# The opening of an attention-and-experts kernel: k's first load in halves on SyncE, the table load ahead of the gate weights, the gate matrix behind the first PV

## The chip, the cores and the metric

The kernel runs on one core of a Trainium2 chip. The metric is the device time of one execution in microseconds (us); a measurement gives the median of several runs. The engines are called PE (TensorE), DVE (VectorE), ACT (ScalarE), POOL (GpSimd) and SP (SyncE, which here only issues DMA).

## The reference

Two stages follow each other. The first is grouped-query attention: 8 batches, 16 query heads, 4 key/value heads, 384 positions, head size 64. The second sends each of the 3072 tokens to one of 16 experts, chosen in two steps (a group of four, then an expert in it).

```python
k = np.repeat(k, group, axis=1); v = np.repeat(v, group, axis=1)
scores = scale * np.matmul(q, k.transpose(0, 1, 3, 2))
attn = np.exp(scores - np.max(scores, axis=-1, keepdims=True))
attn = attn / (np.sum(attn, axis=-1, keepdims=True) + 1e-09)
x = np.matmul(attn, v)          # to (3072 tokens, 1024)
...
g_logits = x @ w_group; g_idx = argmax(g_logits)       # 4 groups
e_logits = xg @ w_expert[g]; e_idx = argmax(e_logits)  # 4 experts of the group
h = np.maximum(x[mask] @ w1[g, e], 0.0)
out[tokens] = (g_w * e_w)[:, None] * (h @ w2[g, e])
```

## The kernel before, in words

The order of the instructions on every engine is written out by hand (`manual_schedule`), and every engine takes its own in that order.

**Attention.** A batch is worked in 24 units: 4 key/value heads ("groups") of 6 key chunks of 64 positions. For unit u, `score(u)` makes eight PE rows of scores (L310) into one of two "s" buffers of PSUM, and ACT writes their exponential as tile `e` (L316). `pv(u)` multiplies `e` with v (L329) and accumulates over the six units of a group in one "o" buffer of PSUM. `run` goes over the units: `score(u + 2)`, `pv(u)`, `tail(u)`, and then what a table of inserts says for this u. `tail` adds pairs of `e` on POOL (L336), has DVE reduce four sums of a group (L343) and evacuates the group's result. Sums over keys are then collected (`collect`, L405), multiplied out on PE (`sums`, L415), inverted (L419), spread (L426) and applied (L435).

**PSUM.** There are two "o" buffers. `ps_tile("o")` takes them in turn; `ps_tile("x")` takes the one that the current group's PV does not use. The first `pv` of a group takes the next buffer in turn, and so waits until whoever holds it has been read out: at the first PV of the second group (u = 6) this is the reader of the last "x" tile before it, which is `gate_matrix_b`'s `wgd` cast on DVE (L239).

**The opening.** Batch 0 can't wait for a DMA transpose, so its q and k are loaded as they are, cast to bf16, transposed on PE against an identity and evacuated (`first_k`, L254; `first_q`, L262; evacuation L245 on ACT or L247 on DVE). SP issues k's first half of the heads (L157), then v (L150), then k's other half of the heads (L173). ACT issues q's first two heads one after the other (L159), then the gate weights of the group and of the experts (L161, L162), and then takes its first exponential on a one-column tile, which brings its table load ahead of the work (L164). POOL issues the other heads of q (L170). While PE waits for data it runs matmuls on ones (`fill`, L273).

**The gate.** `gate_matrix_a` transposes the gate weights on PE (L225) and has DVE copy them to `wg` (L227) and add pairs to `wgs` (L231). `gate_matrix_b` multiplies `wgs` with a folded identity (L236) and has DVE cast the result to `wgd` (L239). Both serve the gate and a guess, from the mean of v, at which expert's weights will be wanted first (`first_guess`, `first_pick` at units 13 and 15: a chain of small DVE operations, L540 to L586, among them L580, which marks the expert). POOL then reads the guess and fetches these weights (`first_fetch`, L560).

After that come, batch by batch, the expert's two matrix products (L622, L633) with the next batch's attention between them.

Of the kernel before, what the change touches and what calls it, by code (L numbers as in the profile page):

```python
# [9 lines left out]
F32 = mybir.dt.float32  # L10
# [4 lines left out]
ACT = mybir.ActivationFunctionType  # L15
# [3 lines left out]
def kernel(  # L19
# [11 lines left out]
    nc = tc.nc  # L31
    P = 128
    B, Hq, S, D = q.shape
# [3 lines left out]
    G, Eg = moe_w1.shape[0], moe_w1.shape[1]  # L37
    F = moe_w1.shape[3]
    NE = G * Eg
    KQ = DM // P  # L40
    KG = KQ // Hkv
# [4 lines left out]
    NC = S // H2  # L46
# [14 lines left out]
    gpool = ctx.enter_context(tc.tile_pool(name="gate", bufs=1))  # L61
# [7 lines left out]
    def ps_tile(which, shape=None, dtype=F32):  # L69
        if which == "x":  # L70
            which = f"o{1 - turn['o']}"
        else:
            turn[which] = 1 - turn[which]
            which += str(turn[which])
        return psum.tile(shape or [P, 2, 512], dtype, name="ps_" + which)
# [3 lines left out]
    NK = Hkv // 2 * NC  # L79
    k16, qraw, vraw, qT, kT = {}, {}, {}, {}, {}  # L80

    def rows(x):
        return x.rearrange("h (p c) d -> (h p) (c d)", c=NC).rearrange("(a p) n -> p a n", p=P)
# [26 lines left out]
    def new_qT(b):  # L110
        qT[b] = xpool.tile([P, KQ * SC, P], BF16, name="qT")

    def new_kT(b):
        kT[b] = xpool.tile([P, NK, P], BF16, name="kT")
# [26 lines left out]
    q0f = stage[:, :4 * NQ].bitcast(F32).rearrange("p (a n) -> p a n", n=NQ)  # L141
    k0f = stage[:, 4 * NQ:8 * NQ].bitcast(F32).rearrange("p (a n) -> p a n", n=NQ)
# [5 lines left out]
    def load_v0(g0, g1):  # L148
        for r in range(2):
            nc.sync.dma_start(out=vraw[0][r * H2:(r + 1) * H2, g0:g1],  # L150
                              in_=v[0, g0:g1].rearrange("h (p c) d -> p h (c d)", c=NC))

    onesb = cpool.tile([P, 4 * P], BF16)
    ones1 = cpool.tile([P, P], BF16)
    nc.vector.memset(ones1, 1.0)
    nc.vector.memset(onesb, 1.0)
    nc.sync.dma_start(out=k0f[:, 0], in_=rows(k[0])[:, 0])  # L157
    for m in range(KG):
        nc.scalar.dma_start(out=q0f[:, m], in_=rows(q[0])[:, m])  # L159
    load_v0(0, 1)  # L160
    nc.scalar.dma_start(out=wraw[:KQ], in_=moe_w_group.rearrange("(a p) g -> a (p g)", p=P))  # L161
    nc.scalar.dma_start(out=wraw[KQ:], in_=moe_w_expert.rearrange("g (a p) e -> (g a) (p e)", p=P))  # L162
    early = gpool.tile([P, 1], F32, name="early")
    nc.scalar.activation(early, onesb[:, :1], ACT.Exp)  # L164
    id128f = cpool.tile([P, P], F32)
    make_identity(nc, id128f)
    id128b = cpool.tile([P, P], BF16)
# [1 line left out]
    for g in range(1, Hkv):  # L169
        nc.gpsimd.dma_start(out=qraw[0][:, KG * g:KG * (g + 1)],  # L170
                            in_=rows(q[0])[:, KG * g:KG * (g + 1)])
# [44 lines left out]
    def index_constants():  # L216
        nc.vector.tensor_copy(out=eidx, in_=eidx_i)
        nc.vector.tensor_scalar(eback, eidx, -1.0, float(NE - 1), op0=ALU.mult, op1=ALU.add)
        nc.vector.tensor_copy(out=pidx, in_=pback_i)

    def gate_matrix_a():
        pe = ps_tile("o")[:, 0, :Eg * 5 * KQ].rearrange("p (e n) -> p e n", e=Eg)
        wv = wraw.rearrange("a (p e) -> a e p", e=Eg)
        for e in range(Eg):
            nc.tensor.transpose(out=pe[:, e], in_=wv[:, e, :],  # L225
                                identity=id128f[:5 * KQ, :5 * KQ])
        nc.vector.tensor_copy(  # L227
            out=wg[:, :, :NW].rearrange("p k (a e) -> p e a k", e=Eg),
            in_=pe.rearrange("p e (a k) -> p e a k", k=KQ))
        pk = pe.rearrange("p e (a g t) -> p t g a e", a=5, t=KG)[:, 0]  # L230
        nc.vector.tensor_add(out=wgs.rearrange("p g (a e) -> p g a e", e=Eg), in0=pk,  # L231
                             in1=wg[:, 1::2, :NW].rearrange("p g (a e) -> p g a e", e=Eg))
# [10 lines left out]
    def evac(eng, out_, in_):  # L243
        if eng is nc.scalar:
            eng.copy(out=out_, in_=in_)  # L245
        else:
            eng.tensor_copy(out=out_, in_=in_)  # L247

    def first_k(gp, which, eng):
        lo = gp * NC  # L250
        pt = ps_tile(which, [P, 16, P], BF16)
        for i in range(NC):
            for s in range(2):
                nc.tensor.transpose(out=pt[s * D:(s + 1) * D, i, :], in_=k16[0][:, lo + i],  # L254
                                    identity=id128b)
        evac(eng, kT[0][:, lo:lo + NC, :], pt[:, :NC, :])

    def first_q(i0, n, which, eng):
        pt = ps_tile(which, [P, 16, P], BF16)
        for i in range(n):  # L260
            a, c = (i0 + i) // SC, (i0 + i) % SC
            nc.tensor.transpose(out=pt[:, i, :], in_=qraw[0][:, a, c * P:(c + 1) * P],  # L262
                                identity=id128b)
        evac(eng, qT[0][:, i0:i0 + n, :], pt[:, :n, :])

    def first_scores():
        new_kT(0)
        new_qT(0)
        warm = ps_tile("o")

        def fill(n):
            for i in range(n):
                nc.tensor.matmul(out=warm[:, i % 2, :], lhsT=onesb[:, :P], rhs=onesb, start=True,  # L273
                                 stop=True)

        for i in range(4):
            nc.tensor.matmul(out=warm[:, i % 2, :P], lhsT=ones1, rhs=ones1, start=True, stop=True)
        fill(6)
        nc.vector.tensor_copy(out=k16[0][:, :NC].rearrange("p c d -> p (c d)"), in_=k0f[:, 0])
        nc.scalar.copy(out=qraw[0][:, 0], in_=q0f[:, 0])  # L280
        nc.vector.tensor_copy(out=qraw[0][:, 1], in_=q0f[:, 1])
        first_k(0, "s", nc.scalar)
        first_q(0, SC, "s", nc.vector)
        first_q(SC, SC, "o", nc.vector)
        fill(2)

    def cast_k():
        nc.gpsimd.tensor_copy(out=k16[0][:, NC:NK].rearrange("p c d -> p (c d)"), in_=k0f[:, 1])
# [378 lines left out]
    def do(f, *a):  # L667
        return lambda: f(*a)

    gate_constants()
    first_scores()
    index_constants()
    at = {0: Attn(0), 1: Attn(1)}
    at[0].start()
    gate_matrix_a()
    state, weights = {}, {}

    new_qT(1)  # L680
# [45 lines left out]
    def second_scale():  # L726
        scale_x(0, 2, spread(0, 2), nc.gpsimd)

    GB = KG * SC
    a = at[0]  # L730
    a.run(0, NU, {
        1: [do(first_q, GB, GB, "x", nc.vector)],
        3: [cast_k],
        4: [gate_matrix_b, do(sum_v, 0, nc.gpsimd)],
        6: [do(collect, 0, 0, 1)],
        7: [do(first_q, 2 * GB, 2 * GB, "x", nc.vector)],
        8: [do(first_k, 1, "x", nc.vector)],
        10: [do(sums, 0, 0, 1, "x"), do(normalise, 0, 0)],
        13: [first_guess],
        14: [do(cast, 0, 0)],  # L740
# [20 lines left out]
    pt = ps_tile("x")  # L761
# [125 lines left out]
    for c in range(SC):  # L887
# [5 lines left out]
        for i, (n0, n1) in enumerate(parts):  # L893
# [8 lines left out]
            for j, (ps, x) in enumerate(halves(c)):  # L902
                eng = nc.scalar if j and i % 2 == 0 else nc.sync
# [5 lines left out]
    with tc.For_i(0, n_left, 1):  # L909
# [27 lines left out]
        x = xb[B]  # L937
        w1, w2 = fetch1(er), fetch2(er)
        m = gpool.tile([P, B, SC, NE], F32, name="pm")
# [51 lines left out]
```

The softmax here doesn't subtract the row's maximum and nothing guards it: scores larger than these inputs give would overflow.

## Time and profile before

| what | value |
|---|---|
| time, median of 3 runs | 366.86 us (366.44 to 367.07) |
| span of the profiled execution | 366.1 us |
| PE busy | 354.2 us (97%) |
| DVE, ACT, POOL busy | 275.7, 230.2, 160.5 us |
| first scores on PE (L310) | from 6.73 us |
| gate weights' transposes (L225) | 7.26 to 7.93 us |
| wgd cast (L239) | 13.28 to 13.69 us |
| k's second load: issue, and POOL's cast of it (L288) | 4.90 us, 14.35 us |

The page gives, for one execution, how long each engine was busy, and a chain of waits: followed back from the last instruction, at each step to what released it. An engine that is busy nearly all the time sets the end where it leads the chain; a wait of another engine costs only where the chain goes through it. Times in views are counted from the start of the span. A line such as L310 is the line of the kernel before.

### The profile page before, as it was taken

Reading aid. Unit: us, or ns where it says so; the run is one execution under the profiler, and the core shown is the slowest. Engines: PE = TensorE matmul, PEld = TensorE weight load, DVE = VectorE, ACT = ScalarE, POOL = GpSimd, SP = SyncE. Lnnn points to the kernel's source line nnn. Section 1 sums busy time; section 2 is a strip of 40 time slices with the busy share of each in tenths; the row PEclk is TensorE's granted clock in tenths of the full one; section 3 lists DMA queues with packets and bytes.
Section 4 is the critical chain, followed back from the end, with each engine's and each line's share of the span. In section 5 each row is a group of like instructions: output and inputs, shape, how many; then the busy total and the mean of one; then the engine's idle time right before and its main releaser. Section 6 shows DMA issues by size and latency. Waiting matters only on the chain.

```text
span 366.1 us, 9424 instructions
## 1 busy us (share of the span) xinstructions
PE 354.2 (97%) x3907; PEld 183.2 (50%) x3907; DVE 275.7 (75%) x506; ACT 230.2 (63%) x300; POOL 160.5 (44%) x127
## 2 busy tenths in 40 slices
PE   8999899999999999999999999999999999999992
PEld 4544455445455455554455445554545545555641
DVE  5689998858988498867989579884998659892230
ACT  5789853759926597267954599265972679544221
POOL 6886890736811476033730377113760258300000
PEclk9999999999999999999999999999999999999999
DMA  8973999999998999999999999989999899999333
GB/s 188 251 118 57 194 181 220 156 208 253 224 163 173 216 252 211 148 209 238 232 208 148 205 249 212 192 175 216 252 210 137 151 211 234 212 213 240 90 85 93
DMA packets 69902, 69.79 MB, mean 191 GB/s; under 512 B 35832, under 2 KB 49944, under 8 KB 69856
## 3 DMA queue, kind: packets, MB, share of 16 engines
q0 software_dynamic: 26864, 41.81, 65.1%
q1 hardware_dynamic: 42320, 26.40, 31.2%
q10 hardware_dynamic: 672, 0.93, 0.9%
q8 instruction: 32, 0.52, 0.5%
q14 instruction: 14, 0.11, 0.1%
HBM read 89.21 MB, written 12.58 MB: 278 GB/s over the span
## 4 chain that ended last, share of the span: by engine, by line
PE 87%; DVE 5%; ACT 2%; POOL 1%; issue 1%; DMA 1%; ACTq 0%
PE ps_o L329 28%; PE ps_s L622 22%; PE ps_s L633 13%; PE ps_s L310 8%; PE ps_o L633 7%; PE ps_o L451 3%; DVE red L343 3%; ACT e L316 2%; PE ps_s L896 2%; PE ps_o L622 1%; POOL e L336 1%; PE ps_o L896 1%; DMA w<-in_q_dram 1%; PE ps_o L415 1%; DVE rb L426 1%
## 5 line engine op out<-in xcount | busy, mean ns | idle before, releaser
L316 ACT ACTIVATE e<-ps_s 128x768 f32<-128x768 f32 x192 | 150.7, 815 | 20.1 <-PE ps_s L310 16.2
L329 PE MATMUL ps_o<-e,v_raw 64*64 64x384 f32 x1536 | 153.3, 483 | 1.4 <-DVE inv L419 1.4
L336 POOL TENSOR_TENSOR e<-e 128x768 f32<-128x768 f32 x64 | 116.4, 1836 | 62.6 <-ACT e L316 43.8
L343 DVE TRANSPOSE_TENSOR_REDUCE red<-e 128x24 f32<-128x768 f32 x128 | 114.1, 946 | 18.3 <-POOL e L336 18.3
L622 PE MATMUL ps_s<-xb,w 128*128 128x384 bf16 x480 | 81.0, 326 | 0.5 <-ACT e L316 0.5
L329 PEld LDWEIGHTS ps_o<-e,v_raw 64*64 64x64 f32 x1536 | 55.4, 133 | 39.7 <-issue 27.4
L622 PEld LDWEIGHTS <-w 128*128 128x128 bf16 x512 | 48.9, 98 | 36.2 <-issue 4.7
L310 PE MATMUL ps_s<-qT,kT 64*64 64x384 bf16 x768 | 63.7, 326 | 0.7 <-ACT e L316 0.2
L626 ACT ACTIVATE hT<-ps_s 128x768 bf16<-128x768 f32 x30 | 24.3, 811 | 61.0 <-PE ps_s L622 58.0
L633 PE MATMUL ps_s<-w,hT 128*128 128x512 bf16 x224 | 50.6, 379 | 0.0
L633 PEld LDWEIGHTS <-hT 128*128 128x128 bf16 x336 | 31.3, 97 | 36.6 <-issue 2.1
L310 PEld LDWEIGHTS <-kT 64*64 64x64 bf16 x768 | 24.2, 105 | 38.9 <-issue 37.1
L689 POOL COPY after<-qT 128x1 bf16<-128x1 bf16 x7 | 2.1, 304 | 79.5 <-DMA qT<-q_raw 78.1
L426 DVE STREAM_TRANSPOSE rb<-inv 128x384 f32<-128x384 f32 x62 | 32.0, 555 | 0.4
L658 ACT ACTIVATE ot<-ps_s,we 128x1024 f32<-128x1024 f32 x14 | 15.6, 1115 | 25.5 <-PE ps_s L633 12.1
L633 PE MATMUL ps_o<-w,hT 128*128 128x512 bf16 x112 | 26.5, 379 | 0.0
L435 DVE TENSOR_TENSOR xT<-xT,rb 128x768 f32<-128x768 f32 x25 | 24.0, 958 | 0.9
L245 ACT CAST xb<-xT 128x768 bf16<-128x768 f32 x27 | 21.7, 830 | 0.0
L461 DVE TENSOR_REDUCE vsum<-v_raw 128x256 bf16<-128x1536 f32 x6 | 16.9, 2815 | 0.0
L379 DVE COPY xT<-ps_o 128x768 f32<-128x768 f32 x18 | 16.5, 919 | 0.0
L660 DVE TENSOR_SCALAR ot<-ps_o,we 128x1024 f32<-128x1024 f32 x7 | 9.0, 1282 | 5.6 <-PE ps_o L633 4.6
L381 ACT COPY xT<-ps_o 128x768 f32<-128x768 f32 x10 | 8.0, 799 | 6.6 <-PE ps_o L329 6.6
(129 smaller groups left out, 201.4 us busy)
## 6 DMA issues: line engine op xcount, KB each, us to landing
w<-in_moe_w_dram POOLq DMA_DIRECT2D x16, 2048.0 KB, 23.4
out_dram<-ot SPq DMA_DIRECT2D x42, 256.0 KB, 6.6
q_raw<-in_q_dram POOLq DMA_DIRECT2D x7, 768.0 KB, 32.1
v_raw<-in_v_dram SPq DMA_DIRECT2D x12, 384.0 KB, 5.3
k<-in_k_dram POOLq DMA_DIRECT2D x7, 192.0 KB, 28.9
out_dram<-ot SPq DMA_DIRECT2D x7, 128.0 KB, 2.3
v_raw<-in_v_dram POOLq DMA_DIRECT2D x2, 384.0 KB, 11.5
w<-in_q_dram POOLq DMA_DIRECT2D x3, 192.0 KB, 7.5
```

Source lines behind the costliest of these rows:

```text
L245: eng.copy(out=out_, in_=in_)
L310: nc.tensor.matmul(out=sT[r * H2:(r + 1) * H2, s, :S], lhsT=kT[b][s * D:(s + 1) * D, slot, ks], rhs=qT[b][s * D:(s + 1) * D, kq * SC:(kq + ...
L316: nc.scalar.activation(e.rearrange("p t (s x) -> p s t x", s=2), sT[:, :, :S].rearrange("p s (t x) -> p s t x", t=2), ACT.Exp, scale=scale)
L329: nc.tensor.matmul(out=oT[t * D:(t + 1) * D, r, :S], lhsT=vraw[b][r * H2:(r + 1) * H2, g, c * D:(c + 1) * D], rhs=self.e[u][r * H2:(r + 1) ...
L336: eng.tensor_add(out=self.e[u], in0=self.e[u], in1=self.e[u + 1])
L343: nc.vector.tensor_reduce(out=reds[self.b][:, g, n].rearrange("p t j -> p (t j)"), in_=self.e[u].rearrange("p t (j x) -> p (t j) x", x=32) ...
L426: nc.vector.transpose(out=rb[:, r].rearrange("p (j x) -> p j x", x=32), in_=inv[b][:, 2 * m + r].unsqueeze(2).to_broadcast([P, NB, 32]))
L435: eng.tensor_mul(out=x, in0=x, in1=rb)
L461: eng.tensor_reduce(out=vsum[b], in_=vraw[b].rearrange("p g (c d) -> p g d c", d=D), axis=AX.X, op=ALU.add)
L622: nc.tensor.matmul(out=h[:, jj, :S], lhsT=w1[:, kq, (f0 + jj) * P:(f0 + jj + 1) * P], rhs=x[:, kq, :], start=(kq == 0), stop=(kq == KQ - 1))
L626: nc.scalar.activation(hT[:, f0:f0 + 2, :], h[:, :, :S], ACT.Relu)
L633: nc.tensor.matmul(out=y[:, nh, :], lhsT=hT[:, f, c * P:(c + 1) * P], rhs=w2[:, f, nh * HALF:(nh + 1) * HALF], start=(f == 0), stop=(f == ...
```

## The change

The change rearranges the opening, so that the first scores need less data ahead of them, and moves what they don't need behind them.

1. k's first load is cut into two halves of three key chunks. SP issues the first half, then q's second head, then the second half; ACT issues only q's first head.
2. ACT's table load stands ahead of the gate weights' loads. By the order of the compiled instructions, the experts' load then waits for the landing of q's first head, with which it shares a semaphore.
3. The cast, transposes and evacuation of k's second half come behind the first two scores, and one filling matmul is left out; the evacuation moves from ACT to DVE for this half.
4. `gate_matrix_a` moves from behind the first two scores to behind the first PV, `gate_matrix_b` from unit 4 to unit 5, and the first transposes of further q heads from unit 1 to unit 2. The index constants (L217 to L219) come behind k's second half.

```diff
-    nc.sync.dma_start(out=k0f[:, 0], in_=rows(k[0])[:, 0])
-    for m in range(KG):
-        nc.scalar.dma_start(out=q0f[:, m], in_=rows(q[0])[:, m])
+    KA = NC // 2
...
+    load_k0(0, KA)
+    for m, eng in enumerate((nc.scalar, nc.sync)):
+        eng.dma_start(out=q0f[:, m], in_=rows(q[0])[:, m])
+    load_k0(KA, NC)
     load_v0(0, 1)
+    early = gpool.tile([P, 1], F32, name="early")
+    nc.scalar.activation(early, ones1[:, :1], ACT.Exp)
     nc.scalar.dma_start(out=wraw[:KQ], in_=moe_w_group...)
     nc.scalar.dma_start(out=wraw[KQ:], in_=moe_w_expert...)
-    early = gpool.tile([P, 1], F32, name="early")
-    nc.scalar.activation(early, onesb[:, :1], ACT.Exp)
...
     def gate_matrix_a():
-        pe = ps_tile("o")[:, 0, :Eg * 5 * KQ]...
+        pe = ps_tile("x")[:, 0, :Eg * 5 * KQ]...
...
-        fill(6)
-        nc.vector.tensor_copy(out=k16[0][:, :NC]..., in_=k0f[:, 0])
+        fill(5)
+        cast_k0(0, KA)
         nc.scalar.copy(out=qraw[0][:, 0], in_=q0f[:, 0])
         nc.vector.tensor_copy(out=qraw[0][:, 1], in_=q0f[:, 1])
-        first_k(0, "s", nc.scalar)
+        first_k(0, KA, "s", nc.scalar)
         first_q(0, SC, "s", nc.vector)
         first_q(SC, SC, "o", nc.vector)
         fill(2)
+        cast_k0(KA, NC)
...
     first_scores()
-    index_constants()
     at = {0: Attn(0), 1: Attn(1)}
     at[0].start()
-    gate_matrix_a()
+    first_k(KA, NC, "o", nc.vector)
+    index_constants()
...
     a.run(0, NU, {
-        1: [do(first_q, GB, GB, "x", nc.vector)],
+        0: [gate_matrix_a],
+        2: [do(first_q, GB, GB, "x", nc.vector)],
         3: [cast_k],
-        4: [gate_matrix_b, do(sum_v, 0, nc.gpsimd)],
+        4: [do(sum_v, 0, nc.gpsimd)],
+        5: [gate_matrix_b],
         6: [do(collect, 0, 0, 1)],
```

More of the change, by code (lines that the diff above doesn't have):

```diff
@@ L156, with load_k0 @@
     nc.vector.memset(onesb, 1.0)
-    nc.sync.dma_start(out=k0f[:, 0], in_=rows(k[0])[:, 0])
-    for m in range(KG):
-        nc.scalar.dma_start(out=q0f[:, m], in_=rows(q[0])[:, m])
+    KA = NC // 2
+    def load_k0(n0, n1):
+        nc.sync.dma_start(out=k0f[:, 0, n0 * D:n1 * D], in_=rows(k[0])[:, 0, n0 * D:n1 * D])
+    load_k0(0, KA)
+    for m, eng in enumerate((nc.scalar, nc.sync)):
+        eng.dma_start(out=q0f[:, m], in_=rows(q[0])[:, m])
+    load_k0(KA, NC)
     load_v0(0, 1)
+    early = gpool.tile([P, 1], F32, name="early")
+    nc.scalar.activation(early, ones1[:, :1], ACT.Exp)
     nc.scalar.dma_start(out=wraw[:KQ], in_=moe_w_group.rearrange("(a p) g -> a (p g)", p=P))
     nc.scalar.dma_start(out=wraw[KQ:], in_=moe_w_expert.rearrange("g (a p) e -> (g a) (p e)", p=P))
-    early = gpool.tile([P, 1], F32, name="early")
-    nc.scalar.activation(early, onesb[:, :1], ACT.Exp)
     id128f = cpool.tile([P, P], F32)
@@ L221, in gate_matrix_a @@
     def gate_matrix_a():
-        pe = ps_tile("o")[:, 0, :Eg * 5 * KQ].rearrange("p (e n) -> p e n", e=Eg)
+        pe = ps_tile("x")[:, 0, :Eg * 5 * KQ].rearrange("p (e n) -> p e n", e=Eg)
         wv = wraw.rearrange("a (p e) -> a e p", e=Eg)
@@ L247, in evac, with first_k @@
             eng.tensor_copy(out=out_, in_=in_)
-    def first_k(gp, which, eng):
-        lo = gp * NC
+    def first_k(n0, n1, which, eng):
         pt = ps_tile(which, [P, 16, P], BF16)
-        for i in range(NC):
+        n = n1 - n0
+        for i in range(n):
             for s in range(2):
-                nc.tensor.transpose(out=pt[s * D:(s + 1) * D, i, :], in_=k16[0][:, lo + i],
+                nc.tensor.transpose(out=pt[s * D:(s + 1) * D, i, :], in_=k16[0][:, n0 + i],
                                     identity=id128b)
-        evac(eng, kT[0][:, lo:lo + NC, :], pt[:, :NC, :])
+        evac(eng, kT[0][:, n0:n1, :], pt[:, :n, :])
     def first_q(i0, n, which, eng):
@@ L277, in first_scores @@
             nc.tensor.matmul(out=warm[:, i % 2, :P], lhsT=ones1, rhs=ones1, start=True, stop=True)
-        fill(6)
-        nc.vector.tensor_copy(out=k16[0][:, :NC].rearrange("p c d -> p (c d)"), in_=k0f[:, 0])
+        fill(5)
+        cast_k0(0, KA)
         nc.scalar.copy(out=qraw[0][:, 0], in_=q0f[:, 0])
         nc.vector.tensor_copy(out=qraw[0][:, 1], in_=q0f[:, 1])
-        first_k(0, "s", nc.scalar)
+        first_k(0, KA, "s", nc.scalar)
         first_q(0, SC, "s", nc.vector)
@@ L285, in first_scores, with cast_k0 @@
         fill(2)
+        cast_k0(KA, NC)
+    def cast_k0(n0, n1):
+        nc.vector.tensor_copy(out=k16[0][:, n0:n1].rearrange("p c d -> p (c d)"),
+                              in_=k0f[:, 0, n0 * D:n1 * D])
     def cast_k():
@@ L731 @@
     a.run(0, NU, {
-        1: [do(first_q, GB, GB, "x", nc.vector)],
+        0: [gate_matrix_a],
+        2: [do(first_q, GB, GB, "x", nc.vector)],
         3: [cast_k],
-        4: [gate_matrix_b, do(sum_v, 0, nc.gpsimd)],
+        4: [do(sum_v, 0, nc.gpsimd)],
+        5: [gate_matrix_b],
         6: [do(collect, 0, 0, 1)],
         7: [do(first_q, 2 * GB, 2 * GB, "x", nc.vector)],
-        8: [do(first_k, 1, "x", nc.vector)],
+        8: [do(first_k, NC, NK, "x", nc.vector)],
         10: [do(sums, 0, 0, 1, "x"), do(normalise, 0, 0)],
```

## The prediction

> **What bounds the kernel now.** I read the page's busy shares first, then the chain of waits in order of time over the first 40 us, then the timelines of single engines around the edited instructions. The page's first part (engine, busy us, share) and the engine shares of its chain:
>
> ```profile
> PE 354.2 (97%) x3907; PEld 183.2 (50%) x3907; DVE 275.7 (75%) x506; ACT 230.2 (63%) x300; POOL 160.5 (44%) x127
> ...
> PE 87%; DVE 5%; ACT 2%; POOL 1%; issue 1%; DMA 1%; ACTq 0%
> ```
>
> TensorE is the bound over the whole span; only the opening stretch has other links. The chain there (start us, us, what):
>
> ```profile
> 0.88 0.41 ACTq L159
> ...
> 1.33 3.80 DMA w<-in_q_dram
> ...
> 5.16 0.70 DVE w L281
> ...
> 6.37 0.43 PE ps_o L273 x2
> 6.80 0.38 PE ps_s L310 x4
> ...
> 12.87 0.38 PE ps_o L236 x2
> ...
> 18.20 1.83 POOL e L336
> ...
> 20.06 1.84 DVE red L343 x2
> ...
> 28.92 1.63 DVE oh_all L580
> ...
> 38.29 0.49 DVE rsum L405
> ...
> 38.82 0.42 PE ps_o L415 x8
> ```
>
> The reader is to see three stretches. Until 6.80 the first scores wait for q's second head (landed at 1.33 + 3.80 = 5.13). From 6.80 to 18.2 PE leads. From 18.2 to 38.8 GpSimd and then VectorE lead without a pause, and PE waits for them. VectorE's timeline in the middle stretch (start, us, engine, line, operation), then PE's where the lead has passed on, then two rows of GpSimd:
>
> ```profile
> 11.11 1.84 DVE L343 TRANSPOSE_TENSOR_REDUCE red<-e 128x24 f32<-128x768 f32 x2 [0.19 <-POOL e L336]
> 13.28 0.41 DVE L239 CAST wgd<-ps_o 64x40 bf16<-64x40 f32 x2 [0.34 <-PE ps_o L236]
> 13.72 1.84 DVE L343 TRANSPOSE_TENSOR_REDUCE red<-e 128x24 f32<-128x768 f32 x2
> 15.60 0.31 DVE L405 TENSOR_REDUCE rsum<-red 128x24 f32<-128x96 f32 x1
> ```
>
> ```profile
> 20.98 0.33 PE L310 MATMUL ps_s<-qT,kT 64*64 64x384 bf16 x4
> 22.14 0.88 PE L329 MATMUL ps_o<-e,v_raw 64*64 64x384 f32 x8 [0.83 <-DVE inv L419]
> ```
>
> ```profile
> 14.35 0.51 POOL L288 CAST w<-w 128x384 bf16<-128x384 f32 x1 [1.07 <-DMA w<-in_k_dram]
> ```
>
> ```profile
> 28.69 1.82 POOL L336 TENSOR_TENSOR e<-e 128x768 f32<-128x768 f32 x1 [1.06 <-ACT xT L381]
> ```
>
> The wgd cast (L239) now stands between the second and the third row reduction; PE has 0.83 us of slack at 22.1; GpSimd's work after 14.35 hangs on k's second load, not on PE.
>
> **What the Trainium skill says.** "PSUM — Partial Sum Buffer", Engine vs sequencer instructions: VectorE's queue is strictly first in, first out. The trace agrees: every VectorE row stands in program order, so what is placed ahead of L239 delays it. "SBUF — State Buffer", Who interferes with whom: VectorE and GpSimd share a port pair that one instruction holds to its end, and the other blocks fully. The trace agrees: L580, a 128x16 operation, took 1.62 us at 28.92, ending with GpSimd's addition of 28.69 to 30.51; the same operation takes 0.23 at 63.27. "DMA: Bandwidth & Descriptors", Queues, rings and completion order: each DMA engine takes turns between the queues that have work. This bears on how far a shorter first transfer helps q's second head.
>
> **The change, part by part.**
>
> *First load.* Before, k's whole load (192 KB, 128 packets) and v's first packets took turns with q's two heads. Now half of k (96 KB) and q's second head share SyncE's queue, and only q's first head takes turns with them. Ahead of the last byte of q's second head stand 96 + 192 + 192 = 480 KB, instead of 192 + 384 and v's share. Traffic between 3 and 4 us ran at 389 GB/s, so 100 to 200 KB fewer are 0.25 to 0.5 us: I estimate a landing near 4.65 (bounds 4.4 and 5.13). But the expert weights' issue on ScalarE now waits for q's first head (landed 0.88 + 3.4 = 4.28 before; I take 4.2), and the first head's cast is queued behind it: 4.2 + 0.32 issue + 0.51 cast = 5.03. Then 0.04 + 0.47 transposes, 0.47 for the second head, 0.43 of filling matmuls: scores at 6.44 instead of 6.80, a gain of 0.36. The second head's own path, 4.65 + 0.69 cast, is through at 5.4 and hidden. The table load ahead of the weights (1.28) is hidden by the wait for q. Bounds of the gain: 0 (second head lands at 5.1, or its cast is held to 5.86 as now) and 0.6.
>
> *Half of k's transposes, behind the first two scores.* They fill the place that the gate matrix (L225, 7.26 to 7.93) has now, beside ScalarE's first exponential; cost nothing. The half casts and evacuations on VectorE lie in its idle time there. One filling matmul less costs or saves nothing, since PE waits for data there.
>
> *Gate matrix behind the first PV.* There PE waits for nothing, so the four transposes are on the path: four weight loads, 0.55, and 0.13 because a score after transposes takes 0.29 instead of 0.16 in the chain: +0.68. The weights, issued some 1.8 us later, took 4.2 us from issue to landing; 4.2 + 4.2 = 8.4 is just ahead of 8.71, where PE wants them (bounds 0 and 0.8 of waiting).
>
> *First q transposes one unit later, second gate product (L236) two places later among the reductions.* By the instruction order the wgd cast now comes behind four reductions instead of two, and the first PV of the second head group, which takes over that PSUM buffer, waits for it. PE: score 2 at 8.07 − 0.36 = 7.71, PV 0 done 8.71, gate matrix 9.26, then 0.29 + 0.65 + 0.16 + 0.65 and q's transposes 0.44: 11.45. From there to the PV: three scores (0.29, 0.16, 0.16), three PVs of 0.65, L236 0.38, one score 0.29 = 3.23, ready at 14.68. VectorE from 11.45: 0.04 + 0.56 copy, 4 x 0.92 reductions, 0.41 cast and about 0.06 of gaps = 4.75, so 16.2. **PE stops for 1.5 us**, and all queued behind it (scores, second q and k transposes) comes at 16.24 instead of 14.34: +1.9.
>
> **How much is absorbed.** The k evacuation on VectorE ends at 18.74 + 1.9 = 20.64; the reduction that starts at 20.06 then starts 0.6 later. PE reaches the PV of 22.14 at 21.31 + 1.9 = 23.21: +1.07, the slack of 0.83 is gone. GpSimd's next addition starts 1.07 later (24.26), is held by VectorE's multiplication to 24.75, ends 26.58; VectorE needs it at 26.59: its shift stays about 0.65. At 27.65 PE now comes by itself, at 28.48; the PV's 0.88 and 0.16 later GpSimd's addition starts at 29.52, 0.05 before L580 at 28.92 + 0.65 = 29.57. It holds it to 31.35, and the pick ends 0.43 later at 31.78 instead of 30.94: +0.84. VectorE runs on to 38.77 + 0.84, PE waits for it there, and no later link before 49.9 has slack, since the chain passes through it. Sum: −0.36 + 0.68 + 1.58 (the stop, less rounding), less 1.06 absorbed = +0.84, **367.70 us**. K's second load may land up to 0.6 us later without setting anything.
>
> **Rivals.** *Worse (368.3):* the second head gains nothing (+0.36), or the gate weights are late by a few tenths; 366.86 + 0.84 + 0.6. For it: the thin margin of 0.3 us at the gate matrix, and the cast L281 that took 0.69 where L279 took 0.36. Against: both would have to be near their bad bounds.
> *Absorbed (366.2 to 367.1):* if GpSimd's addition comes 0.3 us later than in my sum, it misses the pick altogether: VectorE gets 1.39 us back (1.62 − 0.23), +0.65 − 1.39 = −0.74, and PE, +0.83 there less stalls of 0.61 (33.8) and 0.92 (38.8) that vanish, ends at −0.7: 366.2. Or the stop is only half as long and vanishes in the 0.83 of slack: 366.9. For it: 0.05 us decides the order. Against: the addition may as well come earlier.
> *Faster (366.0):* no stop at the PV, and k's second load lands 0.8 us earlier, because v's last early load on SyncE waits for k's half (about 3.5) instead of q's head (4.28); GpSimd's chain and all behind it move 0.8 up: 366.86 − 0.85. Against: reductions of 0.92 each cannot shrink, their inputs are ready, and a queue with 192 KB more ahead of k's second load does not look faster.
>
> **How the numbers follow.** Forecast 0.45 (367.3 to 368.1; 0.28 of it above 367.6, which is +0.2%, and 0.17 below), worse 0.20 (all slower), absorbed 0.20 (0.14 within, 0.06 faster), faster 0.15 (0.12 faster, 0.03 within). Slower 0.48, same 0.34, faster 0.18. Leaving out about half of "faster" below and under half of "worse" above gives 366.1 to 368.7.
>
> **What would show it.** First scores near 6.4; the gate matrix right after the first PV without a wait for DMA; wgd behind four reductions, near 15.8 to 16.2, and about 1.5 us of idle time on PE named for it at the seventh PV; no wait of PE for the reciprocal near 22; L580 still long; the sums product of 38.82 near 39.6. It is wrong if PE doesn't stop at the seventh PV, or if the sums product comes before 38.8.

## The result, and the profile after

| | before | changed |
|---|---|---|
| time, median of 4 runs each | 366.72 us (366.44 to 367.07) | 370.56 us (369.94 to 371.54) |
| ratio | | 1.0107, 95% interval 1.0083 to 1.0131 |
| span of the profiled execution | 366.1 us | 368.1 us |

The change makes the kernel 3.84 us slower, where 0.84 was forecast. First, of the page of the changed kernel, busy time by engine and the chain's shares:

```profile
PE 353.7 (96%) x3891; PEld 183.7 (50%) x3906; DVE 276.3 (75%) x508; ACT 230.0 (62%) x300; POOL 159.6 (43%) x127
...
PE 86%; DVE 7%; ACT 2%; issue 2%; DMA 1%; POOL 0%; ACTq 0%
```

No engine is busy more than 0.6 us longer than before. What is new must be waits, and the chain has them in the opening. The chain of waits of the changed kernel (start us, us, what), with its own line numbers (L321 scores, L340 PV, L231 gate transposes, L354 row reductions, L253 k's evacuation, L594 the last but one operation of the pick, L426 the sums product, L633 the experts' first product):

```profile
0.88 2.98 DMA w<-in_q_dram
3.88 0.34 ACTq L170
...
6.04 0.38 PE ps_s L321 x4
...
8.34 0.86 PE ps_o L340 x4
9.20 1.23 issue
10.43 0.64 PE ps_o L231 x4
...
16.49 1.21 issue
17.70 0.88 PE ps_o L340 x8
...
21.77 0.56 DVE kT L253
22.33 1.74 DVE red L354 x2
...
31.36 1.86 DVE t L594 x2
...
52.34 2.76 PE ps_s L633 x16
```

"issue" is idle time for which the trace has no releaser, so who ended it must come from elsewhere. The reader is to see two such stops of PE, at 9.20 ahead of the gate transposes and at 16.49 ahead of the seventh PV, and behind them VectorE's long part, in which nothing is won back. Who ends the first stop stands in the answer on DMA of the changed kernel (KB each, median us from issue to landing):

```profile
w<-in_moe_w_expert_dram ACTq DMA_DIRECT2D x1, 64.0 KB, 6.5
```

The experts' weights were issued at 3.88 and so landed near 10.4, just ahead of 10.43. Before, they took 4.2 us from 2.47. Who ends the second stop stands in VectorE's timeline (start, us, engine, line, operation):

```profile
13.77 3.55 DVE L354 TRANSPOSE_TENSOR_REDUCE red<-e 128x24 f32<-128x768 f32 x4
17.23 0.37 DVE L245 CAST wgd<-ps_o 64x40 bf16<-64x40 f32 x2
```

Four reductions without a gap, then the `wgd` cast to 17.60, then the PV at 17.70: the order that the prediction read from the program.

### The profile page after: what moved, and what is told of

Its sections match the earlier page's. It is cut to its first block, busy times and chain, and to the rows that moved or that the text cites. A ratio compares the mean times of both kernels' runs of the same rounds, so it can differ in the third digit from the quotient of the medians.

```text
span 368.1 us, 9410 instructions
## 1 busy us (share of the span) xinstructions
PE 353.7 (96%) x3891; PEld 183.7 (50%) x3906; DVE 276.3 (75%) x508; ACT 230.0 (62%) x300; POOL 159.6 (43%) x127
## 4 chain that ended last, share of the span: by engine, by line
PE 86%; DVE 7%; ACT 2%; issue 2%; DMA 1%; POOL 0%; ACTq 0%
PE ps_o L340 28%; PE ps_s L633 22%; PE ps_s L644 13%; PE ps_s L321 8%; PE ps_o L644 7%; PE ps_o L462 3%; DVE red L354 3%; PE ps_s L909 2%; PE ps_o L633 1%; PE ps_o L909 1%; ACT e L327 1%; PE ps_o L426 1%; DMA w<-in_q_dram 1%; DVE vsum L472 1%; DVE rb L437 1%
## 5 line engine op out<-in xcount | busy, mean ns | idle before, releaser
L340 PE MATMUL ps_o<-e,v_raw 64*64 64x384 f32 x1536 | 154.1, 483 | 1.7 <-issue 1.2
L354 DVE TRANSPOSE_TENSOR_REDUCE red<-e 128x24 f32<-128x768 f32 x128 | 113.9, 946 | 16.8 <-POOL e L347 16.8
L633 PE MATMUL ps_s<-xb,w 128*128 128x384 bf16 x480 | 81.0, 326 | 0.2 <-ACT e L327 0.2
L340 PEld LDWEIGHTS ps_o<-e,v_raw 64*64 64x64 f32 x1536 | 56.0, 133 | 39.3 <-issue 28.4
L633 PEld LDWEIGHTS <-w 128*128 128x128 bf16 x512 | 48.9, 98 | 35.9 <-issue 4.4
L321 PE MATMUL ps_s<-qT,kT 64*64 64x384 bf16 x768 | 63.9, 326 | 1.4 <-ACT e L327 1.2
L644 PE MATMUL ps_s<-w,hT 128*128 128x512 bf16 x211 | 49.0, 379 | 0.9 <-issue 0.2
L321 PEld LDWEIGHTS <-kT 64*64 64x64 bf16 x768 | 24.4, 105 | 39.9 <-issue 37.5
L669 ACT ACTIVATE ot<-ps_s,we 128x1024 f32<-128x1024 f32 x14 | 15.6, 1115 | 25.5 <-PE ps_s L644 12.1
L571 POOL DMA_DIRECT2D w<-in_moe_w_dram x8 | 7.3, 916 | 11.3 <-PE ps_s L321 8.0
```

Source lines behind the costliest of these rows:

```text
L321: nc.tensor.matmul(out=sT[r * H2:(r + 1) * H2, s, :S], lhsT=kT[b][s * D:(s + 1) * D, slot, ks], rhs=qT[b][s * D:(s + 1) * D, kq * SC:(kq + ...
L340: nc.tensor.matmul(out=oT[t * D:(t + 1) * D, r, :S], lhsT=vraw[b][r * H2:(r + 1) * H2, g, c * D:(c + 1) * D], rhs=self.e[u][r * H2:(r + 1) ...
L354: nc.vector.tensor_reduce(out=reds[self.b][:, g, n].rearrange("p t j -> p (t j)"), in_=self.e[u].rearrange("p t (j x) -> p (t j) x", x=32) ...
L633: nc.tensor.matmul(out=h[:, jj, :S], lhsT=w1[:, kq, (f0 + jj) * P:(f0 + jj + 1) * P], rhs=x[:, kq, :], start=(kq == 0), stop=(kq == KQ - 1))
L644: nc.tensor.matmul(out=y[:, nh, :], lhsT=hT[:, f, c * P:(c + 1) * P], rhs=w2[:, f, nh * HALF:(nh + 1) * HALF], start=(f == 0), stop=(f == ...
```

## The experiments

In all that follows a time near 370 us is the median of the named kernel's runs, a ratio is to the kernel before on the same chip, with its 95% interval, and any other number in us is from the named kernel's own trace. The kernels were run on different chips, so they are compared by their ratios.

**The kernel before, again.** No edit.

> The kernel before, unchanged, taken once more with a profile on the same chip as the three runs below. Both theories expect 366.5 to 367.2 us, and in the trace the same links: first scores at 6.7 to 6.8, gate matrix near 7.3 without a wait, the sums product of the second pair of groups near 38.8. If its span in the trace is about 365 instead of 366.1, the difference between the traces of before and after (2.0 us) understates the difference of the medians (3.8 us) only because the first trace was a long execution.

366.87 us, ratio 0.9991 (0.9977 to 1.0005), span 364.7: the time is the same, but the trace differs from the one that the prediction was worked from (span 366.1). Its chain of waits, where GpSimd's last addition hands over to VectorE:

```profile
17.27 1.79 POOL e L336
19.08 1.84 DVE red L343 x2
```

The reduction that started at 20.06 in the first trace starts at 19.08 here. K's second load landed at 13.3 instead of 14.3, and with it GpSimd's cast, its sum of v and its addition moved up by one microsecond. VectorE's k evacuation ends at 18.62 in this trace, so what comes later than that has 0.46 us of slack and not the 1.3 of the first trace. The first traced execution was a long one: it took 367.74 us, where the three timed runs took 366.44 to 367.07. The second took 366.39, a little under its median. All traces are compared with this one from here on.

**Gate weights ahead of the table load.** The changed kernel, with

```diff
-    nc.scalar.activation(early, ones1[:, :1], ACT.Exp)
     nc.scalar.dma_start(out=wraw[:KQ], ...)
     nc.scalar.dma_start(out=wraw[KQ:], ...)
+    nc.scalar.activation(early, ones1[:, :1], ACT.Exp)
```

> The changed kernel with one part undone: the gate weights are issued ahead of ACT's table load again, so the experts' load waits for nothing. Theory A (the late weights are the larger part): the gate matrix follows the first PV without the 1.23 us wait for DMA, and all behind it comes 1.2 us or more earlier; about 369.0 us or less. Theory B (the stop at the seventh PV behind four reductions is the larger part, and runs in series with the rest): the stop of about 1.2 us stays, since it hangs on DVE's order behind q's transposes, which move with PE; still at most 1.2 us gained. Rival C (the weights' wait only hides DVE's delay): no gain, 370.3 to 370.8, with a longer stop at the seventh PV.

369.88 us, ratio 1.0082 (1.0062 to 1.0101). The weights, issued at 1.94, landed at 6.24, and the stop at the gate transposes is gone. PE's timeline of this kernel has in its place:

```profile
8.89 0.86 PE L340 MATMUL ps_o<-e,v_raw 64*64 64x384 f32 x4 [0.33 <-DMA v_raw<-in_v_dram]
...
16.99 0.88 PE L340 MATMUL ps_o<-e,v_raw 64*64 64x384 f32 x8 [1.24 <-issue]
```

The second half of the first PV now waits for v's second part, which landed at 8.85 (8.29 in the changed kernel, 7.29 in the kernel before), and the stop at the seventh PV is as long as it was. So the weights' wait is real, but of its 1.23 us only 0.7 come back.

**First q transposes and second gate product in their old units.** The changed kernel, with

```diff
         0: [gate_matrix_a],
-        2: [do(first_q, GB, GB, "x", nc.vector)],
+        1: [do(first_q, GB, GB, "x", nc.vector)],
         3: [cast_k],
-        4: [do(sum_v, 0, nc.gpsimd)],
-        5: [gate_matrix_b],
+        4: [gate_matrix_b, do(sum_v, 0, nc.gpsimd)],
```

> The changed kernel with q's first further transposes at unit 1 and the second gate product at unit 4 again; the gate matrix stays behind the first PV and the table load stays ahead. Theory B: the wgd cast stands behind two reductions again, the stop of PE at the seventh PV is gone (under 0.2 us), and 0.5 to 1.2 us are won: 369.4 to 370.1. Theory A: the wait for the weights stays whole at 1.2 us, so at least 368.5 remains. If the stop's removal is absorbed by a later wait, 370.3 to 370.8.

370.82 us, ratio 1.0115 (1.0092 to 1.0138). The stop at the seventh PV is gone from the trace, and the time is no better. GpSimd's second addition starts at 15.04 (13.00 in the changed kernel), and PE's granted clock (the part of its full clock that it was given) was 0.67 and 0.50 in the stretches from 10 to 12 and from 12 to 14 us. VectorE's timeline has k's evacuation:

```profile
21.78 0.56 DVE L253 COPY kT<-ps_o 128x768 bf16<-128x768 bf16 x1 [0.62 <-PE ps_o L260]
```

It ends at 22.34, where it ended at 22.33 in the changed kernel. So what was saved at the seventh PV was lost on PE's own path before GpSimd came in, and GpSimd's late chain held the reduction behind it up by 0.17 more. Two experiments further down take up the slow clock.

**The halves alone.** The kernel before with the new load order on SyncE and k's halves, and all the rest (weights, gate transposes, units) as before, but for the index constants and the filling matmul that is left out, which come along:

```diff
+    load_k0(0, KA)
+    for m, eng in enumerate((nc.scalar, nc.sync)):
+        eng.dma_start(out=q0f[:, m], in_=rows(q[0])[:, m])
+    load_k0(KA, NC)
...
+    first_k(KA, NC, "o", nc.vector)
     index_constants()
     gate_matrix_a()
```

> Only k's load in halves and q's second head on SyncE remain, with k's second transposes behind the first two scores; table load behind the weights, gate matrix ahead of the first PV, second product at unit 4, first further q transposes at unit 1, all as before. The scores start 0.7 us earlier than before. If that gain passes through, 366.0; if GpSimd's and VectorE's work from 14 to 39 us sets the rest, 366.5 to 367.0. A time above 367.5 would say that the halves themselves cost, for example through v's later landing.

367.47 us, ratio 1.0013 (1.0004 to 1.0023). The first scores start 0.9 us earlier (5.7), as the change wants it, and then the gain is lost. In its chain of waits:

```profile
1.80 4.97 DMA w<-in_k_dram
...
18.13 1.78 POOL e L347
19.91 0.03 issue
19.94 1.84 DVE red L354 x2
```

K's second half lands at 6.79 and PE waits for it, so that the third score comes at 8.07, 0.1 later than before. K's second load lands at 14.2, 0.9 later, GpSimd works its chain off 0.86 later, and VectorE's reduction follows. The gain at the scores is real and worth nothing alone: the kernel is 0.5 us slower.

**The order alone.** The kernel before with its own loads, and with gate transposes, first q transposes and second gate product where the change puts them:

```diff
-        pe = ps_tile("o")[:, 0, :Eg * 5 * KQ]...
+        pe = ps_tile("x")[:, 0, :Eg * 5 * KQ]...
...
-    gate_matrix_a()
...
-        1: [do(first_q, GB, GB, "x", nc.vector)],
+        0: [gate_matrix_a],
+        2: [do(first_q, GB, GB, "x", nc.vector)],
         3: [cast_k],
-        4: [gate_matrix_b, do(sum_v, 0, nc.gpsimd)],
+        4: [do(sum_v, 0, nc.gpsimd)],
+        5: [gate_matrix_b],
```

> The kernel before with its own loads, and only the three moves in the order: gate transposes behind the first PV, first q transposes a unit later, second gate product a unit later. Theory (the waits add up, and each is its own): no wait for gate weights or v, gate transposes on TensorE's path +0.77, seventh PV ready near 15.0 and stopped to 16.2 behind four reductions (+1.2), k's evacuation on VectorE ends near 20.9, the first reduction of the third group then starts 1.8 later than the 19.08 of the undisturbed kernel before: about 368.6, ratio 1.0045 to 1.0055. Rival (most of the loss hangs on the loads): no stop at the seventh PV once the weights are early, +0.3 at most, ratio 1.000 to 1.001. Rival (the absorption of the prediction): +1.2, ratio 1.003.

Ratio 1.0045 (1.0031 to 1.0058), or 1.65 us; the medians (368.86 and 366.86) and the spans of the traces (366.7 and 364.7) lie 2.0 apart. The chain of waits, before's line numbers:

```profile
8.95 0.60 PE ps_o L225 x4
9.55 0.29 PE ps_s L310 x4
...
14.66 0.32 PE ps_s L310 x4
...
16.18 0.88 PE ps_o L329 x8
...
20.26 0.56 DVE kT L247
20.81 1.74 DVE red L343 x2
```

The gate transposes follow the first PV without a wait, the seventh PV is ready at 14.98 and runs at 16.18, and the reduction starts 1.73 later than 19.08. So the order costs 1.65 to 2.0 us with every load in time, as its theory had it. Of the changed kernel's 3.84 this leaves some 2 us to the loads and what they set off.

**The sum of v a unit later.** Meant to move GpSimd's sum of v behind its next addition, in the kernel before:

```diff
-        4: [gate_matrix_b, do(sum_v, 0, nc.gpsimd)],
+        4: [gate_matrix_b],
+        5: [do(sum_v, 0, nc.gpsimd)],
```

> The kernel before with GpSimd's sum of v one unit later, behind the addition of the sixth unit instead of ahead of it. Theory (GpSimd's chain from the addition at 11.3 to the one that ends at 19.06 is the bound of the kernel before there, by 0.46 over VectorE's k evacuation): the reduction of 19.08 starts near 18.6, span and median 0.4 to 0.5 shorter, ratio 0.9987. Rival (TensorE or VectorE bounds there anyway): no change, ratio 1.000. Rival (the sum of v, 3.4 us, collides with the next additions or comes late for the guess that reads it near 22.8): slower, ratio 1.001 or more.

Ratio 1.0002 (0.9987 to 1.0018). A miss of mine: the additions stand in units 1, 3, 7 and 9, so that none lies between units 4 and 5, and GpSimd's order is unchanged. It says nothing on the theory, but its trace is a third one of the order of before (366.52 us): k's second load landed at 12.8, VectorE's k evacuation ends at 18.31 and the reduction starts at 18.58, so the slack is 0.27 here.

**Six filling matmuls again.** The changed kernel with `fill(6)` for `fill(5)`.

> The changed kernel with six filling matmuls again instead of five. Theory (the fill costs or saves nothing): ratio as the changed kernel's, 1.010 to 1.011, scores within 0.1 of the changed kernel's. Rival (the idle stretch at 4.1 that the missing fill leaves keeps TensorE's clock low, so that transposes and fills run at half speed in part of the runs): no fill of 0.5 us at 5.3, first scores near 5.7, ratio 1.008.

371.17 us, ratio 1.0108 (1.0072 to 1.0144), the changed kernel's own. The fill costs or saves nothing that five runs with so wide an interval could show. In the trace the theory missed: the first scores come at 6.55, not within 0.1 of the changed kernel's 6.04, since the last two filling matmuls took 1.06 us instead of 0.60. The rival, by which it is the missing fill that makes them slow, fails as well: they are slow here with six fills, and took 1.06 with five in the two experiments above that start from the changed kernel. Why they are slow in some executions the traces don't show.

**Old units, and the sum of v a unit later.** The third experiment's edit with the sum's, which by the same mistake adds nothing: it is the third experiment once more.

> The changed kernel with first q transposes and second gate product in their old units, and GpSimd's sum of v one unit later. Theory (with the old units alone the gain of 1.2 at the seventh PV was lost to GpSimd's chain, which the late first scores had pushed back): addition right behind the k cast, the first reduction of the third group waits for k's evacuation instead, near 21.2, about 369.4, ratio 1.007. Rival (what was lost with the old units was lost to the clock of TensorE or to the wait for the gate weights): ratio as with the old units alone, 1.011.

370.85 us, ratio 1.0099 (1.0069 to 1.0130). PE's work by stretches in its trace (start:end, length, busy us and instructions of each engine, granted clock, DMA share, GB/s):

```profile
8.00:10.00 2.00, 0.72 (x6) 0.05 (x2) 0.00 (x0) 0.64 (x1) 1.12 (x1) 1.00 1.19 270
10.00:12.00 2.00, 1.72 (x20) 1.08 (x21) 0.68 (x2) 0.74 (x1) 0.68 (x1) 1.00 1.19 260
12.00:14.00 2.00, 2.00 (x22) 0.86 (x23) 1.56 (x3) 0.88 (x2) 0.00 (x0) 0.52 1.19 271
14.00:16.00 2.00, 2.00 (x24) 0.86 (x20) 0.74 (x1) 0.90 (x2) 1.67 (x1) 0.62 1.20 268
```

PE is busy all the time from 12 to 16, at little more than half its clock: a PV takes 1.28 in the chain instead of 0.65. The stretch follows the 1.56 us in which PE waited for the gate weights. By the clock it costs (1 − 0.52) × 2 + (1 − 0.62) × 2 = 1.7 us, an estimate, and more than the 1.2 that the old units save at the seventh PV. The chain agrees:

```profile
10.28 0.64 PE ps_o L231 x4
...
21.81 0.56 DVE kT L253
22.37 1.74 DVE red L354 x2
```

From the gate transposes to the end of k's evacuation it is 12.09 us here, and 10.42 in the next experiment's kernel, which has the same order and no slow stretch. GpSimd holds nothing up at 22.37. Over its ten runs the time goes with the clock: the two with a mean of 0.996 or more took 368.8 us, the three at 0.988 or less 371.9 to 372.9. So in this kernel a slow stretch behind the wait for the weights costs as much again. That the wait brings the stretch about is likely, as the next experiment has neither, but not proven: a few executions of the kernel before have a mean clock of 0.989 to 0.991 too, and took 368.9 to 370.0 us.

**Both waits away at once** (g1_first_and_back). The changed kernel with the edits of the second and third experiments together.

> The changed kernel with the gate weights issued ahead of the table load and with first q transposes and second gate product in their old units: TensorE waits neither for the weights nor at the seventh PV, and what is left of the change is the load order, k's halves and the gate transposes behind the first PV. Theory (the two waits and the half-speed stretches of TensorE that follow the wait for the weights make most of the loss; left are v's late landing, +0.9, and the gate transposes, +0.77, less 0.5 at the scores): no stretch at half speed, first reduction of the third group near 20.5, about 368.2, ratio 1.003 to 1.005. Rival (GpSimd's chain holds everything as with the old units alone): 369.5 or more, ratio 1.008 or more.

368.20 us, ratio 1.0037 (1.0018 to 1.0056), as its theory had it, and no slow stretch of PE in the trace. PE's timeline has one wait left in the opening behind the third score, and the lead is GpSimd's again:

```profile
8.84 0.86 PE L340 MATMUL ps_o<-e,v_raw 64*64 64x384 f32 x4 [0.68 <-DMA v_raw<-in_v_dram]
```

```profile
18.45 3.58 POOL L347 TENSOR_TENSOR e<-e 128x768 f32<-128x768 f32 x2
```

Together the two edits bring 1.0107 − 1.0037 = 0.70%, or 2.6 us; one alone brought 0.25%, the other nothing. So the gains don't add up from the single edits. With the weights first, the stop at the seventh PV stayed as long as it was; with the old units, the weights' wait stayed, and in both traces of that kernel the half-speed stretch took what was saved.

**v taken off SyncE's queue.** The last kernel with the second of v's two first parts issued on ScalarE behind q's first head:

```diff
-    load_v0(0, 1)
+    load_v0(0, 1, (nc.sync, nc.scalar))
```

> The changed kernel with gate weights first and the old units, as in g1_first_and_back, and with the second half of v's first load issued on ScalarE, behind q's first head, instead of last on SyncE. Theory (v's landing at 8.8 behind k's second half on SyncE's queue is a wait of its own, 0.7 to 0.9): v lands before 7, TensorE's wait for it is gone, 0.6 to 0.8 shorter than g1_first_and_back, ratio near 1.0015. Rival (all these loads share the same bandwidth, and what v gains, k's halves, the heads of q or the gate weights lose): ratio stays at 1.003 or more.

368.16 us, ratio 1.0040 (1.0027 to 1.0053): no gain. In PE's and in GpSimd's timeline:

```profile
8.20 0.88 PE L340 MATMUL ps_o<-e,v_raw 64*64 64x384 f32 x8 [0.57 <-DMA v_raw<-in_v_dram]
```

```profile
15.67 0.51 POOL L299 CAST w<-w 128x384 bf16<-128x384 f32 x1 [1.65 <-DMA w<-in_k_dram]
```

The part on ScalarE landed at 4.83, but the one left on SyncE at 8.16, so the theory's "before 7" failed for it; the first PV still ends 0.6 earlier (9.08 against 9.70). In this trace that is lost again at k's second load, which landed 1.4 later (15.6 against 14.3), as the rival has it. But the last experiment below has the same loads, and there v's part on SyncE landed at 7.20, PE didn't wait for it, and k's second load landed at 14.2. So the missing gain is shown by five runs, and its cause by one trace that another doesn't repeat: it stays open.

**Towards a faster kernel.** Three edits to the kernel before: the sum of v behind the addition of unit 7, where there is one; the same with q's second head on SyncE behind k's whole load; and the first with GpSimd's read of the picked index (`pick`) one unit earlier (h1_pick_first), ahead of its addition of unit 19. The third edit, which contains the first:

```diff
-        4: [gate_matrix_b, do(sum_v, 0, nc.gpsimd)],
+        4: [gate_matrix_b],
...
-        7: [do(first_q, 2 * GB, 2 * GB, "x", nc.vector)],
+        7: [do(sum_v, 0, nc.gpsimd), do(first_q, 2 * GB, 2 * GB, "x", nc.vector)],
...
+        18: [do(pick, 0)],
...
     def first_fetch():
-        pick(0)
         transposed(1)
```

> The kernel before with GpSimd's sum of v really behind the addition of unit 7 (the additions stand in units 1, 3, 7 and 9; between units 4 and 5 there was none). Theory (GpSimd's chain bounds the kernel before there by 0.46): addition of unit 7 near 15, reduction of 19.08 at 18.6, and if the pick then comes 0.1 ahead of GpSimd's addition at 27.5 its 1.62 us shrink to 0.23: 0.4 to 1.5 shorter, ratio 0.996 to 0.999. Rival (TensorE or VectorE bounds there anyway, or the additions of units 9 and 13 come later): ratio 1.000 or more.

> The kernel before with only q's second head on SyncE, behind k's whole first load and ahead of v, and with the sum of v behind the addition of unit 7. Theory (q's second head sets the first scores, v and the gate weights still land in time): second head lands 0.2 to 0.4 earlier, first scores near 6.3, both gains add: ratio 0.995 to 0.998. Rival (what k gains q's second head takes from v or from the gate weights, as in the changed kernel): first scores earlier but TensorE waits for weights or v by as much, ratio as with the sum of v alone.

> The kernel before with the sum of v behind the addition of unit 7, and GpSimd's read of the picked index placed one unit earlier, so that GpSimd waits for VectorE's pick ahead of its addition of unit 19 and can't hold the port against it. Theory (the shared port makes L580 1.6 to 1.9 us long, and VectorE leads there): L580 takes 0.23, the index is ready 1.5 earlier, TensorE's waits of 0.62 near 33 and 0.9 near 38 shrink, 0.5 to 1.5 less than with the sum alone, ratio 0.995 to 0.997. Rival (the addition of unit 19, now behind the pick, comes late for the row reductions, or TensorE bounds there): ratio 0.998 to 1.000. A higher ratio would say that GpSimd's addition is what the end waits for.

The sum alone: 366.59 us, ratio 0.9987 (0.9978 to 0.9997). In its traced execution the first scores came at 7.16, 0.48 later than in the trace of before, and the reduction at 19.03 all the same: GpSimd no longer leads there, and that was worth 0.5 us. With q's second head on SyncE as well: 0.9997 (0.9986 to 1.0007). That head landed at 5.10, no earlier than from ScalarE (4.99). With only half of k's load ahead of it, as in the changed kernel, it landed at 4.37. The early read: 365.35 us, ratio 0.9951 (0.9933 to 0.9970), **the fastest kernel of the study**. VectorE's timeline at the pick, GpSimd's row behind it, and PE's first named wait behind 6 us, in this kernel:

```profile
27.91 0.23 DVE L580 TENSOR_SCALAR oh_all<-key,km 128x16 f32<-128x16 f32 x1
28.18 0.17 DVE L583 SCALAR_TENSOR_TENSOR t<-eidx,oh_all 128x16 f32<-128x16 f32 x1
...
28.47 2.69 DVE L343 TRANSPOSE_TENSOR_REDUCE red<-e 128x24 f32<-128x768 f32 x3
```

```profile
29.59 1.82 POOL L336 TENSOR_TENSOR e<-e 128x768 f32<-128x768 f32 x1 [2.98 <-DVE red L343]
```

```profile
47.68 2.76 PE L622 MATMUL ps_s<-xb,w 128*128 128x384 bf16 x16 [0.64 <-ACT e L316]
```

L580 took 1.88 us with the sum alone and takes 0.23 here: GpSimd stands idle for 2.98 us, until it has read the index that VectorE writes behind L580, and its addition, which ran beside L580 before, starts only at 29.59. PE's waits near 33 and 38 (0.62 and 0.92 with the sum alone) are gone.

**All of it on the changed kernel's load order.** The kernel with v partly on ScalarE, and these two moves.

> The same, with the sum of v behind the addition of unit 7 and the read of the picked index a unit earlier, the two moves of h1_pick_first. Theory (with v and the weights in time, the earlier first scores pay for the gate transposes on TensorE's path, and nothing else is left of the change): as h1_pick_first, within 0.3 us, ratio 0.995. Rival (the halves still delay what follows): 0.5 or more longer than h1_pick_first, ratio 0.9965 or more. Below 0.9945 the load order would be worth keeping.

365.63 us, ratio 0.9976 (0.9963 to 0.9990). The medians of the two lie 0.3 us apart, but each was set against its own runs of before, and by the ratios this one is 0.25% behind, with intervals that just overlap. The traces are as close as the medians (spans 363.7 and 363.5). So the theory (as h1_pick_first) holds by medians and traces, and the rival (slower) by the ratio; which is right stays open, but a gain from the new load order does not show. GpSimd's cast of k's second load, at 15.67 in the experiment on v, comes earlier here with the same loads:

```profile
14.27 0.51 POOL L299 CAST w<-w 128x384 bf16<-128x384 f32 x1 [0.78 <-DMA w<-in_k_dram]
```

## Why the prediction was wrong

*The direction and the places* were right: slower, through the gate transposes on PE's path and a stop at the seventh PV behind four reductions. *Filling matmul, table load, half transposes at nothing*: not contradicted for the fill. Behind the table load ScalarE stood idle for 1.44 us until q's first head had landed, so it was hidden. The half transposes are not in the changed kernel's chain; in the halves-alone kernel PE waited 0.79 us for the cast of k's second half.

*"First load", −0.36*: measured −0.64 (6.04 against 6.68). The path was the one in the sum, from q's first head over the weights' issue and the head's cast on ScalarE, but the head landed at 3.85 and not at 4.2. Q's second head landed at 4.37, the good bound.

*"Gate matrix", +0.68*: 0.77 by the chains, and right.

*"PE stops for 1.5 us" (1.58 in the sum)*: 1.21 with the new loads and 1.20 without; the PV behind the stop then takes 0.88 instead of 0.65, which the sum didn't have.

*The gate weights' wait, 0, with bounds 0 and 0.8*: **the first term that failed.** It was 1.23. The landing was worked from 4.2 us, the duration of an earlier issue into other traffic; issued at 3.88 the same 64 KB took 6.5 us (6.3 to 6.5 in the four traced kernels with this order). Even at its old place, near 2.47, it took 4.2 to 5.1 us in the traces with that order. The sum left a margin of 0.3 us, and the upper bound was no bound, since nothing of before showed such a load issued late.

*v's landing*: **a term that was missing**, +0.89. The sum counted the bytes ahead of q's second head on SyncE's queue and not those ahead of v on the same queue. The share is read from the chain (8.34 to 9.20, with v's second part landed at 8.29) and named as a wait for v in the two kernels with the weights first and this load order. Moving part of v to ScalarE shortened nothing, and why is open.

*"How much is absorbed", 1.06*: **the second that failed.** From k's evacuation 3.71 later (22.33 against 18.62) to the experts' first product 3.39 later (52.34 against 48.95), 0.32 was absorbed. The slack of 1.3 us at the reduction came from an execution in which k's second load landed a microsecond late; 0.46 and 0.27 are what the two later traces of that order show. The execution of the first trace stands out by its time, 367.74 us against a median of 366.86. The pick was blocked as forecast, but one operation later, at L594 with 1.86 us; the one that was named took 0.25. By tenths of a microsecond it went as the sum has it, and not as its rival "absorbed".

In sum, against the second trace: −0.64 + 0.89 + 1.23 + 0.77 + 1.21 + 0.23 = 3.69, less 0.32 absorbed, is 3.4, and so far apart are the two spans (368.1 and 364.7). The medians lie 3.84 apart; the traced execution of the changed kernel was the fastest of its four (369.94 us). For the rest of 0.4 a candidate is the half-speed stretch: it is in the traces of three kernels that keep the weights' wait, and two of the changed kernel's other executions had a mean clock of 0.992 and 0.991 (0.994 in the traced one). It is not in the one traced execution, so that this stays open.

## What to carry to other kernels

A load that is moved behind others has no known duration: bound its landing by what is queued and in flight then, for every reader of that queue, and not by what it took at its old place. Slack that one trace shows may belong to that execution; set its time against the median, and take a second before counting on it. And undoing one of two waits can bring nothing because of what the other still sets off, so undo them together before calling either harmless.

## What the runs showed of the hardware

- *PE at half its clock behind a wait much shorter than 3.4 us, but not behind every one.* "TensorE: Matmul & The Clock Gate", Part 1: The HAM clock gate, says that the clock halves after an idle window of about 3.4 us that runs freely. The half and the length agree: in the windows shown above PE lost 1.7 us at a clock of one half, a stretch of 3.4 us by that estimate. The idle time doesn't: 1.56 us in one piece came ahead of it there, with PE busy for 0.72 of the 2 us from 8 to 10, and only 0.93 us in the two other traces that have such a stretch (the third experiment's and that with six fills). The wait of 1.23 us in the changed kernel's trace and the stops of 1.2 us at the seventh PV had none behind them, so the length of a wait alone doesn't decide.
- *One port, two signs.* The section of the SBUF page that the prediction names was borne out by taking the collision away: an operation on 128x16 took 0.23 us instead of 1.6 to 1.9. Which one of two neighbours is hit depends on tenths: L580 in the kernel before, the one behind it (L594, 1.86 us) in the changed kernel.
- *A load on another engine's queue brings no clear gain.* "DMA: Bandwidth & Descriptors", Issuing engines are not separate DMA queues, says that another issuing engine saves only the time of the issue. The runs don't contradict it and don't show it either: with v partly on ScalarE the time stayed (ratio 1.0040 against 1.0037), but k's second load took 10.5 us from issue to landing in one trace and 9.0 in the other, against 8.8 with v on SyncE. The turns between queues that the prediction takes from the same page fit the trace of before, where from 3 to 4 us 221 packets of one queue and 77 of another moved; whose turn it was when, it doesn't tell.
